# Dynamic convolution and gated projection on one core: another order of TensorE's products, and 32-column tiles for one of them, placed between the two halves of the convolution

## The chip, the cores and the metric

The kernel runs on one core of a Trainium2 chip. The metric is the device time of one execution in microseconds, median of several runs; lower is better. Engines are named as in the profile: PE is TensorE, PEld its weight loads, DVE VectorE, ACT ScalarE, POOL GpSimd; SP issues DMAs.

## The reference

Batch 8, sequence 4224, width 192, all float32. Cut to what is computed:

```
w   = softmax(weight_gen, axis=-1)               # (8, 4224, 8 heads, 7 taps)
x1[b,s,h,:] = sum_k w[b,s,h,k] * xpad[b,s+k,h,:] # causal, 24 channels per head
gate = sigmoid(sum_j conv_w[j,c] * x1pad[b,s+j,c])   # 5 taps per channel, causal
out  = (gate * (x1 @ w_val)) @ w_out             # 192 x 192 each
```

## The kernel before, in words

The sequence is cut into groups of 120 positions (88 in the first, 56 in the last); two groups make a *pair*, and 19 pairs, counted by `q`, go through three steps, one round apart. All work is recorded at hand-written times: `at(t, fn)` puts an entry on a list, and the list sorted by time is the program's order. In round `q`, `st(off, ...)` records at `when(q) + off`; a round is 24.5 units long (18 for `q` = 2). An entry's time is only its place in the order; on the chip every engine takes its own instructions in that order and waits on semaphores.

In round `q`:

- *Convolution of pair q* (`bank`, L343): eight banks of sixteen products, four banks for each group. Each product has 126 rows and 32 columns of weights, in one of four column positions. Two banks go to the PSUM tile `ps[0]`, two to `ps[1]`. ScalarE copies each bank out (`evac`, L358: `S`, `ringB`, `ringA` twice). GpSimd's DMAs (`move`) then bring rows from `S` to their places in `ringA` and `ringB`.
- *First taps of pair q* on ScalarE (`tap0`, L384), late in the round.
- *Gate and value of pair q-1*. VectorE adds four taps of `aA` and four of `aB` (`tap`, L388); ScalarE applies the sigmoid to each (`sigm`, L393). PE makes the value products in four parts, here by the size of tile (rows x columns of PE's array): `wvm_` (L415, 128 x 32, to `ps[2]`), `wva_` (L420, 128 x 128, two pieces, to `ps[0]` and `ps[1]`), `wvd_` (L426, 64 x 64, to `ps[2]`), `wvb_` (L432, 64 x 128, added to `wva_`'s pieces). VectorE multiplies gate and value (`gv`): L439 reads `ps[0]`, then `ps[1]`; L444 and L447 read `ps[2]`.
- *Output of pair q-2* in four pieces: `omA` (L455, 128 x 128) and `omB` (L464, 64 x 128) add up in one PSUM tile, ScalarE copies it out (`oev`, L470), SP stores it (`store`, L478). Piece 0 is written to `ps[3]` early in the round, the others late. The tile of a piece is `bk[i]`; `tA`, `tB`, `tE` are the places of `omA`, `omB` and `oev`.

The softmax weights are made in parts of 2048 positions, about one part in two rounds. One kind of round, called *X* here, has the exponential on ScalarE (L223: a load of another function table, then the function; after it the sigmoid L393 needs a table load too), and sum, reciprocal and product on VectorE (L227 to L249). The other kind, *Y*, has SP's copies of halo rows (`halo`, L241, after the product L249), ScalarE's four copies that spread the weights (`spread`, L261, after the halo copies have landed), and maximum and difference on VectorE (L215, L219). SP also issues per round 18 loads of these weights for the next pair (L317) and, by turns, four stores (L272) or four loads (L206).

What writes into a PSUM tile waits for the engine that read its last contents. In the order before, `ps[1]` and `ps[2]` carry the last two output pieces, so these wait for `gv`; the next round's convolution needs `ps[0]` from `gv` and `ps[1]` from a copy of `oev`.

Of the kernel before, what the change touches and what calls it, by code (L numbers as in the profile page):

```python
# [16 lines left out]
def tile_dynconv_gated_moe(  # L17
# [91 lines left out]
    def at(t, fn, *args):  # L109
        plan.append((t, len(plan), fn, args))  # L110
# [72 lines left out]
    class Softmax:  # L183
# [29 lines left out]
        def max(self):  # L213
            w, m = self.own()
            nc.vector.tensor_reduce(out=m, in_=w, axis=AX.X, op=ALU.max)  # L215
# [287 lines left out]
    def when(q):  # L503
        return WHEN[q] if q < 4 else WHEN[3] + TP * (q - 3)
# [99 lines left out]
    for p in parts[3:]:  # L604
        q = next(q.q for q in pairs if p.use < q.s + q.n)
# [17 lines left out]
    for q, pr in enumerate(pairs + [None, None]):  # L623
        p1 = pairs[q - 1] if 1 <= q <= NP else None
        p2 = pairs[q - 2] if q >= 2 else None
        t = when(q)

        def st(off, fn, *args):
            at(t + off, fn, *args)

        if pr:
            ng = len(pr.g)
            order = [(gi, kind) for gi in range(ng) for kind in (3, 2, 0, 1)]
            for i, (gi, kind) in enumerate(order):
                st(0.8 * i, pr.bank, gi, kind, i % 4)
                st(0.8 * i + 0.9, pr.evac, gi, kind, i % 4)
            m0 = [(k, u) for k in (4, 5) for u in range(2)]
            m1 = [(k, u) for u in range(2) for k in range(4)]
            for i, (k, u) in enumerate(m0 + m1):
                late = 0.8 * (4 * (ng - 1) + (1, 2, 3)[i // 4]) + (0.91 if q else 1.5)  # L640
                st(late + 0.001 * i, pr.move, k, u)
            for g in range(2):
                st((17.5, 11.0, 14.8)[min(q, 2)], pr.halo, g)
            st((17.6, 11.1, 15.9)[min(q, 2)], pr.tap0, 0, 0)
            st((17.7, 11.2, 17.0)[min(q, 2)], pr.tap0, 0, 1)
            st((17.8, 11.3, 19.6)[min(q, 2)], pr.tap0, 1)
        if q + 1 < NP:
            nx = pairs[q + 1]
            for gi, g in enumerate(nx.g):
                if q >= 1:  # L650
                    if g.n == NB:
                        st((0.0, 7.2)[gi], g.load_x, nc.gpsimd)
                    else:
                        st(7.2, lambda g=g: nc.gpsimd.memset(g.xb[:, :, :], 0.0))
                        st(7.3, g.load_x, nc.gpsimd)
                for i, (p, w, lo, hi) in enumerate(g.segments()):
                    tt = max(t + (3.5, 7.0)[gi], p.ready + 0.001 * (1 + gi))
                    if q == 0:
                        tt = 30.5 if p is s0 else (34.0, 37.0)[gi]
                    assert p.ready < tt < when(q + 1), (q, gi, tt, when(q + 1))  # L660
                    at(tt, g.load_t, p, w, lo, hi, (nc.sync, nc.scalar)[i % 2 if q == 0 else 0])
        if p1:
            E = range(p1.pieces)
            for j in range(1, KC):
                st((2.6 if q > 1 else 8.0) + 2.1 * (j - 1) * (1 if q > 1 else 0.1), p1.tap, 0, j)
                st((11.4 if q > 1 else 8.5) + 1.2 * (j - 1) * (1 if q > 1 else 0.1), p1.tap, 1, j)
            st(11.5 if q > 1 else 8.9, p1.sigm, 0)
            st(16.4 if q > 1 else 9.0, p1.sigm, 1)
            st(6.5, p1.wvm_)
            st(10.2, p1.wvd_)  # L670
            for e in E:
                st(8.2 + 0.8 * e, p1.wva_, e)
                st((15.0 if q > 1 else 10.3) + 0.8 * e, p1.wvb_, e)
                st((15.9 if q > 1 else 10.4) + 0.8 * e, p1.gv, 0, e)
                st((17.6 if q > 1 else 10.5) + 0.1 * e, p1.gv, 1, e)
        if p2:
            J2 = [(e, k) for e in range(p2.pieces) for k in range(2)]
            bk = (3, 3, 1, 2)
            tA = (2.9, 17.5, 18.9, 20.2)
            tB = (3.0, 16.7, 21.4, 22.0)  # L680
            tE = (3.35, 18.8, 21.95, 22.7)
            for i, (e, k) in enumerate(J2):
                af = tA[i] < tB[i]
                st(tA[i], p2.omA, e, k, bk[i], af)
                st(tB[i], p2.omB, e, k, bk[i], not af)
                st(tE[i], p2.oev, e, k, bk[i])
                st(tE[i] + 0.01, p2.store, e, k, nc.sync)
# [29 lines left out]
```

## Time and profile before

| | |
|---|---|
| median of 3 runs | 536.47 us (536.35 to 538.43) |
| the profiled execution's own time | 530.59 us |
| its span, first to last instruction | 528.8 us |
| mean granted TensorE clock | 0.942 |
| PE busy | 454.5 us, 86% |
| DVE busy | 427.1 us, 81% |
| ACT busy | 313.6 us, 59% |
| POOL busy | 317.3 us, 60% |

The profile is of one execution that took 530.59 us, 5.88 us less than the median. The span leaves out what lies before the first and after the last instruction (1.8 us). A share of busy time is an average over stages: the first 137 us fill the pipeline, then come 14 whole rounds, then the last short ones.

### The profile page before, as it was taken

The numbers are of one execution on the slowest core, as the hardware profiler recorded it, in microseconds if no ns is written. First come the engines' busy times: TensorE is split into PE (matmuls) and PEld (weight loads), VectorE is DVE, ScalarE is ACT, GpSimd is POOL, SyncE is SP. The second block draws the span as 40 slices with busy tenths as digits, with TensorE's granted clock in tenths as the row PEclk, the third lists the DMA queues.
The fourth block names the chain that finished last, engine by engine and source line by source line (L and its number), as shares of the span: only waits on it lengthen the run. The fifth ranks groups of instructions, "written<-read, shape, count | busy, mean of one in ns | idle before, by whom it ended". The sixth has DMA issues, their size and how long they took to land.

```text
span 528.8 us, 15980 instructions
## 1 busy us (share of the span) xinstructions
PE 454.5 (86%) x6546; PEld 330.2 (62%) x6546; DVE 427.1 (81%) x342; ACT 313.6 (59%) x433; POOL 317.3 (60%) x554
## 2 busy tenths in 40 slices
PE   7030674969999899999999999999998999999996
PEld 3030552556858485858676776768584868586584
DVE  6988346898979896999799979888995979595960
ACT  6432364658585748485858675767767575545532
POOL 9878256667474839293949382938566565807400
PEclk9565697879999999999999999999999999999999
DMA  7796749986979797879797978797797858654344
GB/s 222 212 307 187 202 110 254 244 234 175 248 218 281 196 270 195 270 195 269 208 288 201 267 199 263 202 259 220 219 254 220 256 149 251 177 165 100 92 113 111
DMA packets 86743, 112.42 MB, mean 213 GB/s; under 512 B 19133, under 2 KB 73796, under 8 KB 86542
## 3 DMA queue, kind: packets, MB, share of 16 engines
q1 hardware_dynamic: 62988, 70.86, 46.9%
q0 software_dynamic: 22560, 38.13, 28.1%
q10 hardware_dynamic: 1122, 2.40, 1.4%
q8 instruction: 52, 0.85, 0.6%
q14 instruction: 21, 0.17, 0.1%
HBM read 59.63 MB, written 42.43 MB: 193 GB/s over the span
## 4 chain that ended last, share of the span: by engine, by line
PE 44%; issue 15%; DMA 14%; POOL 13%; DVE 7%; ACT 5%; SPq 2%; ACTq 0%; POOLq 0%; DVEq 0%
PE ps L343 15%; PE ps L455 10%; POOL xt L286 6%; PE ps L464 6%; PE ps L420 5%; POOL ringA L366 4%; DMA xt<-in_x_dram 3%; PE ps L415 3%; PE ps L432 3%; POOL ringB L368 2%; DMA ringA<-S 2%; DMA tb<-z 2%; DMA ringB<-S 2%; PE ps L426 2%; DVE aB L447 1%
## 5 line engine op out<-in xcount | busy, mean ns | idle before, releaser
L343 PE MATMUL ps<-tb,xt 126*32 126x120 f32 (+2 forms) x4608 | 148.0, 286 | 62.3 <-DMA tb<-z 26.8
L343 PEld LDWEIGHTS ps<-tb,xt 126*32 126x32 f32 x4608 | 134.9, 115 | 74.5 <-issue 33.4
L388 DVE SCALAR_TENSOR_TENSOR aA<-ringA,wf,aA 128x1920 f32<-128x1920 f32 (+2 forms) x76 | 157.3, 2070 | 15.9 <-ACT aA L384 13.7
L286 POOL DMA_DIRECT2D xt<-in_x_dram x272 | 158.4, 597 | 17.8 <-DMA xt<-in_x_dram 5.0
L368 POOL DMA_DIRECT2D ringB<-S x76 | 42.1, 559 | 139.0 <-ACT ringB L358 113.0
L455 PE MATMUL ps<-wf,aA 128*120 128x192 f32 (+2 forms) x576 | 108.7, 336 | 5.9 <-DVE aB L447 3.9
L455 PEld LDWEIGHTS ps<-wf,aA 128*120 128x120 f32 (+2 forms) x576 | 91.2, 186 | 20.2 <-DVE aB L447 9.0
L470 ACT COPY ot<-ps 120x768 f32<-120x768 f32 (+2 forms) x72 | 56.0, 802 | 66.2 <-PE ps L464 55.2
L366 POOL DMA_DIRECT2D ringA<-S x152 | 82.0, 547 | 21.6 <-DMA ringB<-S 9.0
L388 DVE SCALAR_TENSOR_TENSOR aB<-ringB,wf,aB 128x960 f32<-128x960 f32 (+2 forms) x76 | 86.9, 1143 | 1.9
L439 DVE TENSOR_TENSOR aA<-ps,aA 128x960 f32<-128x960 f32 (+2 forms) x36 | 39.3, 1130 | 52.7 <-PE ps L432 33.1
L420 PE MATMUL ps<-ringA,wva 128*128 128x480 f32 (+2 forms) x144 | 61.8, 571 | 0.0
L464 PE MATMUL ps<-wf,aB 64*120 64x192 f32 (+2 forms) x576 | 59.7, 335 | 0.9 <-ACT ot L470 0.9
L358 ACT COPY S<-ps 128x480 f32<-128x480 f32 (+2 forms) x36 | 19.9, 552 | 63.2 <-PE ps L343 46.5
L464 PEld LDWEIGHTS ps<-wf,aB 64*120 64x120 f32 (+2 forms) x576 | 46.5, 182 | 16.8 <-issue 15.2
L358 ACT COPY ringA<-ps 128x480 f32<-128x480 f32 (+2 forms) x72 | 36.2, 554 | 33.7 <-PE ps L343 33.7
L384 ACT ACTIVATE aA<-ringA,wf 128x960 f32<-128x960 f32 (+2 forms) x38 | 39.2, 1033 | 22.9 <-DMA ringA<-S 22.7
L420 PEld LDWEIGHTS ps<-ringA,wva 128*128 128x128 f32 x144 | 25.8, 189 | 35.7 <-issue 22.2
L261 ACT COPY zt<-wt 128x512 f32<-128x512 f32 (+3 forms) x36 | 30.9, 936 | 5.7 <-DMA wt<-wt 3.2
L432 PE MATMUL ps<-ringB,wvb 64*128 64x480 f32 (+2 forms) x144 | 33.5, 581 | 0.0
L415 PE MATMUL ps<-ringA,wvm 128*32 128x480 f32 (+2 forms) x304 | 33.5, 537 | 0.0
L393 ACT ACTIVATE aA<-aA 128x1920 f32<-128x1920 f32 (+2 forms) x19 | 32.1, 1690 | 1.0 <-DVE aA L388 0.9
(62 smaller groups left out, 361.1 us busy)
## 6 DMA issues: line engine op xcount, KB each, us to landing
xt<-in_x_dram POOLq DMA_DIRECT2D x272, 94.5 KB, 3.7
out_dram<-ot SPq DMA_DIRECT2D x68, 360.0 KB
tb<-z SPq DMA_DIRECT2D x235, 74.4 KB
z<-zt SPq DMA_DIRECT2D x28, 306.0 KB
wt<-in_weight_gen_dram SPq DMA_DIRECT2D x28, 224.0 KB
ringA<-S POOLq DMA_DIRECT2D x136, 30.0 KB, 3.5
tb<-z SPq DMA_DIRECT2D x69, 52.1 KB
wt<-wt SPq DMA_DIRECT2D x9, 294.0 KB
```

What stands on the lines that cost most here:

```text
L286: eng.dma_start(out=self.xb[0:G * NW, j, 0:D], in_=src)
L343: nc.tensor.matmul(out=pa[Q * c:Q * c + Q, n * l:n * l + n], lhsT=g.xb[0:k, LH * u + l, C * h:C * h + Q], rhs=t[:, (LH * u + l) // LQ, PAD ...
L358: nc.scalar.copy(out=dst, in_=pa)
L366: nc.gpsimd.dma_start(out=ringA[q:q + h, LH * u:LH * u + LH, p0:p0 + n], in_=St[p:p + h, :, 0:n])
L368: nc.gpsimd.dma_start(out=ringB[HD * u + q:HD * u + q + h, :, p0:p0 + n], in_=St[p:p + h, :, 0:n])
L388: nc.vector.scalar_tensor_tensor(out=a, in0=self.src(g, j), scalar=cw[:, g, j:j + 1], in1=a, op0=ALU.mult, op1=ALU.add)
L415: nc.tensor.matmul(out=ps[2][c:c + Q, i, 0:self.w * self.pieces // 2], lhsT=wvm[:, Q * k:Q * k + Q], rhs=self.half(0, u, i), start=True, s ...
L420: nc.tensor.matmul(out=self.v01(e)[:, u], lhsT=wva, rhs=self.A(e, u), start=True, stop=False)
L432: nc.tensor.matmul(out=self.v01(e)[:, u], lhsT=wvb[hs], rhs=self.Bt(e)[hs], start=False, stop=True, tile_position=(HD * u, 0))
L455: nc.tensor.matmul(out=ps[b][0:n, u, D * t:D * t + D], lhsT=g[:, u, t], rhs=woa, start=first and t == 0, stop=not first, skip_group_check= ...
L464: nc.tensor.matmul(out=ps[b][0:n, u, D * t:D * t + D], lhsT=g[hs, t], rhs=wob[hs], start=first and t == 0, stop=not first, skip_group_chec ...
L470: nc.scalar.copy(out=ots[0:n, 2 * e + k], in_=ps[b][0:n, :, 0:2 * D])
```

## The change

In rounds from `q` = 2 on, the products of the value and output stand elsewhere in the order. `wvm_` goes from after the convolution to between its two groups. Output piece 0 goes from between the two groups to after `wva_`; its copy and store go with it. `wvb_` follows it, then `wvd_`. The last three output pieces have their three `omA` first and their three `omB` after, and two of them use `ps[0]` and `ps[1]` in place of `ps[1]` and `ps[2]`. No instruction is added or removed, apart from how they group.

```diff
-            st(6.5, p1.wvm_)
-            st(10.2, p1.wvd_)
+            st(2.9 if q > 1 else 6.5, p1.wvm_)
+            st(10.0 if q > 1 else 10.2, p1.wvd_)
             for e in E:
                 st(8.2 + 0.8 * e, p1.wva_, e)
-                st((15.0 if q > 1 else 10.3) + 0.8 * e, p1.wvb_, e)
+                st((9.8 if q > 1 else 10.3) + 0.01 * e, p1.wvb_, e)
                 st((15.9 if q > 1 else 10.4) + 0.8 * e, p1.gv, 0, e)
...
-            bk = (3, 3, 1, 2)
-            tA = (2.9, 17.5, 18.9, 20.2)
-            tB = (3.0, 16.7, 21.4, 22.0)
-            tE = (3.35, 18.8, 21.95, 22.7)
+            bk = (3, 3, 0, 1)
+            tA = (9.5, 18.0, 18.9, 20.2)
+            tB = (9.6, 21.6, 21.0, 21.3)
+            tE = (9.65, 21.65, 21.05, 21.35)
```

On PE, in a whole round of the middle, from the convolution's second group on (`tb1`; `ps0` to `ps3` are the PSUM tiles). Before:

```order
L343 MATMUL ps0_91<-tb1_64,xt0_72 32x120 x32
L343 MATMUL ps1_92<-tb1_64,xt0_72 32x120 x32
L415 MATMUL ps2_93<-ringA_75,wvm_86 32x480 x8
L420 MATMUL ps0_91<-ringA_75,wva_83 128x480 x2
L420 MATMUL ps1_92<-ringA_75,wva_83 128x480 x2
L426 MATMUL ps2_93<-ringB_76,wvd_85 64x480 x4
L432 MATMUL ps0_91<-ringB_76,wvb_84 128x480 x2
L432 MATMUL ps1_92<-ringB_76,wvb_84 128x480 x2
L464 MATMUL ps3_94<-wf_88,aB1_80 120x192 x4
L455 MATMUL ps3_94<-wf_88,aA_78 120x192 x4
L455 MATMUL ps1_92<-wf_88,aA_78 120x192 x4
L455 MATMUL ps2_93<-wf_88,aA_78 120x192 x4
```

And in the change, the same place:

```order
L343 MATMUL ps1_92<-tb1_64,xt0_72 32x120 x32
L420 MATMUL ps0_91<-ringA_75,wva_83 128x480 x2
L420 MATMUL ps1_92<-ringA_75,wva_83 128x480 x2
L455 MATMUL ps3_94<-wf_88,aA_78 120x192 x4
L464 MATMUL ps3_94<-wf_88,aB1_80 120x192 x4
L432 MATMUL ps0_91<-ringB_76,wvb_84 128x480 x2
L432 MATMUL ps1_92<-ringB_76,wvb_84 128x480 x2
L426 MATMUL ps2_93<-ringB_76,wvd_85 64x480 x4
L455 MATMUL ps3_94<-wf_88,aA_78 120x192 x4
L455 MATMUL ps0_91<-wf_88,aA_78 120x192 x4
L455 MATMUL ps1_92<-wf_88,aA_78 120x192 x4
L464 MATMUL ps0_91<-wf_88,aB1_80 120x192 x4
```

Output piece 0 (the first L455 and L464 here) came from between the convolution's groups; L415 went there. Before, the round ends with L464 to `ps1` and `ps2`; now with L464 to `ps0`, `ps1` and `ps3`.

On ACT, in a round of kind X, around the table loads. Before:

```order
L470 COPY ot_82<-ps3_94 120x768
L358 COPY S_77<-ps0_91 128x4x120
L358 COPY ringB_76<-ps0_91 128x4x120
L358 COPY ringA_75<-ps1_92 128x4x120 x2
L223 ACT_TABLE_LOAD
L223 ACTIVATE wt2_67<-wt2_67 128x2x896
L393 ACT_TABLE_LOAD
L393 ACTIVATE aA_78<-aA_78 128x1920
```

And in the change:

```order
L358 COPY S_77<-ps0_91 128x4x120
L358 COPY ringB_76<-ps0_91 128x4x120
L358 COPY ringA_75<-ps1_92 128x4x120 x2
L223 ACT_TABLE_LOAD
L223 ACTIVATE wt2_67<-wt2_67 128x2x896
L470 COPY ot_82<-ps3_94 120x768
L393 ACT_TABLE_LOAD
L393 ACTIVATE aA_78<-aA_78 128x1920
```

The copy of output piece 0 (L470) moved from ahead of the second group's copies to between the exponential and the sigmoid's table load. In a round of kind Y it moved to between the four copies L261 and the sigmoid.

On SP, where a round of kind X ends and one of kind Y begins. Before:

```order
L206 DMA wt2_67<-in_weight_gen_dram 32x2x896 x4
L478 DMA out_0_dram<-ot_82 120x2x384 x3
L241 DMA wt1_66<-wt1_66 112x2x336
L241 DMA wt1_66<-wt1_66 12x2x336
L478 DMA out_0_dram<-ot_82 120x2x384
L317 DMA tb0_63<-z0_97 14x4x238
```

And in the change:

```order
L478 DMA out_0_dram<-ot_82 120x2x384
L206 DMA wt2_67<-in_weight_gen_dram 32x2x896 x4
L478 DMA out_0_dram<-ot_82 120x2x384 x3
L241 DMA wt1_66<-wt1_66 112x2x336
L241 DMA wt1_66<-wt1_66 12x2x336
L317 DMA tb0_63<-z0_97 14x4x238
```

The store of output piece 0 moved from ahead of the 18 loads L317 to behind them. The order on DVE and on POOL is the same in both kernels.

## Rows read from the trace of the kernel before

**Rows 1.** Busy time in fourteen rounds: us, PE, PEld, DVE, ACT, POOL; clock; DMA.

```profile
137.15:489.55 352.40, 342.87 (x5042) 250.07 (x5040) 304.12 (x219) 228.99 (x309) 213.38 (x377) 1.00 0.80 223
```

**Rows 2.** Timeline of PE, one whole round (start, us, operation, count of records).

```profile
365.68 3.88 PE L343 MATMUL ps<-tb,xt 126*32 126x120 f32 x128
369.48 1.57 PE L455 MATMUL ps<-wf,aA 128*120 128x192 f32 x8
370.98 0.92 PE L464 MATMUL ps<-wf,aB 64*120 64x192 f32 x8
371.83 3.89 PE L343 MATMUL ps<-tb,xt 126*32 126x120 f32 x128
375.51 1.82 PE L415 MATMUL ps<-ringA,wvm 128*32 128x480 f32 x16
377.26 3.49 PE L420 MATMUL ps<-ringA,wva 128*128 128x480 f32 x8
380.68 1.04 PE L426 MATMUL ps<-ringB,wvd 64*64 64x480 f32 x8
381.64 1.88 PE L432 MATMUL ps<-ringB,wvb 64*128 64x480 f32 x8
383.36 0.82 PE L464 MATMUL ps<-wf,aB 64*120 64x192 f32 x8
384.11 4.48 PE L455 MATMUL ps<-wf,aA 128*120 128x192 f32 x24
388.51 1.57 PE L464 MATMUL ps<-wf,aB 64*120 64x192 f32 x16
390.01 1.24 PE L343 MATMUL ps<-tb,xt 126*32 126x120 f32 x36
```

**Rows 3.** Timeline of PE, near the end: three output pieces without a wait.

```profile
513.71 4.17 PE L455 MATMUL ps<-wf,aA 128*120 128x192 f32 x24
```

**Rows 4.** PE by line, fourteen rounds: busy, mean ns, idle before and releasers.

```profile
L343 PE MATMUL ps<-tb,xt 126*32 126x120 f32 x3584 | 110.1, 278 | 3.8 <-issue 3.6
L455 PE MATMUL ps<-wf,aA 128*120 128x192 f32 x448 | 84.9, 337 | 5.8 <-DVE aB L447 3.9 <-DVE aA L439 1.5
```

**Rows 5.** Timeline of DVE, a round X and the round Y after it.

```profile
257.18 2.22 DVE L439 TENSOR_TENSOR aA<-ps,aA 128x960 f32<-128x960 f32 x2 [2.86 <-PE ps L432]
...
267.44 8.97 DVE L388 SCALAR_TENSOR_TENSOR aA<-ringA,wf,aA 128x1920 f32<-128x1920 f32 x4
...
282.03 2.22 DVE L439 TENSOR_TENSOR aA<-ps,aA 128x960 f32<-128x960 f32 x2 [0.72 <-ACT aA L393]
...
290.18 4.47 DVE L388 SCALAR_TENSOR_TENSOR aA<-ringA,wf,aA 128x1920 f32<-128x1920 f32 x2
```

**Rows 6.** Timeline of ACT, a round X.

```profile
249.58 1.02 ACT L358 COPY ringA<-ps 128x480 f32<-128x480 f32 x2 [0.80 <-PE ps L343]
...
251.91 1.70 ACT L223 ACTIVATE wt<-wt 128x1792 f32<-128x1792 f32 x1
253.62 1.28 ACT L393 ACT_TABLE_LOAD   x1
254.92 1.80 ACT L393 ACTIVATE aA<-aA 128x1920 f32<-128x1920 f32 x1
```

**Rows 7.** Timeline of ACT, the round Y of rows 2.

```profile
371.95 0.81 ACT L470 COPY ot<-ps 120x768 f32<-120x768 f32 x1 [1.32 <-PE ps L464]
373.93 0.56 ACT L358 COPY S<-ps 128x480 f32<-128x480 f32 x1 [1.17 <-PE ps L343]
```

**Rows 8.** Timelines of DVE, SP and ACT, another round Y.

```profile
163.41 2.03 DVE L249 TENSOR_TENSOR wt<-wt,mx 128x1792 f32<-128x1792 f32 x1
...
168.24 2.49 SPq L241 DMA_DIRECT2D wt<-wt  x2
...
175.94 3.77 ACT L261 COPY zt<-wt 128x512 f32<-128x512 f32 x4 [2.56 <-DMA wt<-wt]
```

**Rows 9.** ACT by line, fourteen rounds: busy, mean ns, idle before and releasers.

```profile
L261 ACT COPY zt<-wt 128x512 f32<-128x512 f32 (+3 forms) x24 | 21.2, 959 | 5.1 <-DMA wt<-wt 2.6 <-DMA out_dram<-ot 1.3 <-DVE aB L388 1.2
```

## The prediction, before the run

> **What bounds the kernel now.** I began with busy time by stretch. In the fourteen whole rounds between 137.15 and 489.55 us PE is busy 342.87 of 352.40 us at a clock of 1.00, which is 2.4 GHz; DVE 304.12, ACT 228.99 [rows 1]. So PE is the bound there, with 9.5 us idle, and a round takes 352.40 / 14 = 25.17 us. The timeline of PE then shows what a round is made of [rows 2]: its rows overlap by less than 0.1 us, so a step's length is the distance to the next row's start. In microseconds: convolution 3.80, output piece 0 in 1.50 + 0.85, convolution 3.68, value products 1.75 (L415), 3.42 (L420), 0.96 (L426), 1.72 (L432), output 0.75, 4.40, 1.50. Sum 24.33: the round without a stall. 14 x 24.33 = 340.6, so stalls cost 11.8 us in all. PE by line names most of them [rows 4]: 5.8 us before L455, on DVE, and 3.8 us in the convolution, nearly all "issue", a wait whose cause the trace doesn't show. DVE is not far behind: from the gate products of a round X at 257.18 to the start of the next taps at 267.44 it needs 10.26; taps take until 281.31 (282.03 less 0.72 idle), 13.87; in the round Y gate products and softmax take 290.18 - 282.03 = 8.15 [rows 5]. For X and Y together that is 10.26 + 8.15 + 2 x 13.87 = 46.15, or 23.08 a round.
>
> **What a change of tiling costs.** The 24 records of L455 near the end took 4.17 - 0.08 (the overlap) = 4.09 [rows 3]; 8 records with a change before and after took 1.50 [rows 2]. So 16 cost 2.59, 8 cost 1.295, and a change on both sides 0.205. L464 says the same: 16 records 1.50, 8 records 0.85, so 0.65 and 0.20; and after L432, which has the same tiling, 8 records took 0.75: one change, 0.10 at each end. The convolution takes 0.12 less when L415, also of 32 columns, follows (3.68 against 3.80).
>
> Per round I count nine changes before, and six after: into L420, L464, L426, L455, L464, L343. The new round, in its order: convolution 3.68; L415 1.75 - 0.10 = 1.65; convolution 3.75 (3.80 less an entry, not separately shown, between 0 and 0.10, taken as 0.05); L420 3.32; L455 1.40; L464 0.75; L432 1.72 (its change moves from entry to exit); L426 0.96; three L455 4.09; three L464 3 x 0.65 + 0.20 = 2.15. Sum 23.47. Against 24.33 that is 0.86 less: 0.55 for tilings, and 0.31 because three L455 took 4.40 and not 4.09: the third waited for `ps[2]`, which L447 reads last. The last pieces now use `ps[0]` and `ps[1]`, which L439 frees before L447 is done with `ps[2]`.
>
> **What takes the place of PE.** If PE ran without a stall, a round would be 23.47. It doesn't, because the copy of output piece 0 now stands on ACT directly ahead of the sigmoid. ACT takes its work in order: before, it sat idle 1.32 us for piece 0 and 1.17 for the copy behind it [rows 7].
>
> Round X. L464 of piece 0 ends 3.68 + 1.65 + 3.75 + 3.32 + 1.40 + 0.75 = 14.55 after the round's start. Its copy started 371.95 - 371.83 = 0.12 after that point before [rows 2, 7]: 14.67. ACT would be free by about 13.3: the second convolution ends at 9.08, then 1.02 of copies, 1.28, 1.70 and some 0.2 of signals [rows 6]. The copy (0.81 [rows 7], less some 0.09 by which rows of one engine overlap) lets the next instruction go at 15.39, the table load (1.28, plus 0.02) at 16.69, the sigmoid (1.80) at 18.49, and the first L439 (half of 2.22, with a signal at each end) at 19.68. PE reaches the second L455 of the late three, in `ps[0]`, at 14.55 + 1.72 + 0.96 + 0.10 + 1.30 = 18.63. It waits 1.05 and loses 0.10 in loading weights anew: the round takes 24.62. Before, exponential, table load and sigmoid followed each other without that copy [rows 6].
>
> Round Y. DVE starts the gate products of X at 18.53 and is ready for the next after 10.26 + 13.87 = 24.13, which is 18.04 in Y. ACT is in time: L261 takes 3.77 [rows 8] and may start at 10.2, after the convolution's copies; if it starts by 11.7, copy and sigmoid are done by 18.0. So L439's first half ends at 19.2, PE waits 0.57 and 0.10: 24.14.
>
> X and Y together take 48.76, before 2 x 24.33 = 48.66. The tilings' gain is thus paid back where both kinds of softmax work occur. Rounds without it exist: L261 has 24 records, four to a round [rows 9], so of fourteen rounds six are Y, six X and two plain. Plain rounds have neither wait: 23.47, a gain of 0.86 each. The last softmax part has 8 rows a partition in place of 16, so in its Y DVE is early: about 0.6 gained. Sum: five pairs +0.5, the last X +0.3, its Y -0.6, two plain -1.7: **-1.5 us**.
>
> **Stalls.** Of 5.8 us before L455, 3.9 ended with L447 [rows 4]. That place is gone: after L447 comes only `wvm_`, in the next round. Where the cause was a late sigmoid, the wait returns at L439; I take half of the 5.8 as gone, **-2.9**, with 0 and -3.9 as ends. "Issue" stays: 3.8, perhaps less where PE would wait for DVE anyway (0.67 in Y): **-0.5**, with 0 and -1.5.
>
> **Start and end.** Until 137 us PE waits for loads; nothing is taken there. The last three short rounds have fewer changes too, 0.55 and less each: **-1.0**, with 0 and -1.6.
>
> SP's loads for the next pair start sooner, because piece 0's store no longer stands ahead of them; they landed in time before, so nothing is taken. ACT's first copies of a round now wait for nothing new; PE's first bank waits for the copy of piece 2, which takes 0.12 + 0.81 beside the 1.40 of L464 behind it.
>
> **Sum:** -1.5 - 2.9 - 0.5 - 1.0 = -5.9. On the profiled execution's own 530.59 that is 524.7; the median of the runs is 536.47, 5.88 higher, so I set the difference against the median: **530.5**, 1.1% less.
>
> **A rule weighed.** The trace has the sigmoid's table load begin 0.01 after the exponential ends, and the sigmoid 0.02 after the load [rows 6]; I price the switch at 1.28. The Trainium skill, ScalarE: Activation LUTs, section What ACT_TABLE_LOAD costs, gives 1.28 for the load and adds a drain of 1.38 to every switch. With that, as an estimate from its figures, six rounds X would each be 1.38 longer, and the sum +2.4 in place of -5.9. No row here has such a gap.
>
> **Rivals.**
>
> *All of it arrives.* ACT isn't late, PE never waits for L439: 14 x 0.86 + 5.8 + 1.0 = 18.8 less, 517.7. For it: PE bounds the stretch [rows 1]. Against: ACT waited in order for piece 0 [rows 7]. It would need the table load to pass a waiting copy. By the Trainium skill, TensorE: Matmul & The Clock Gate, ScalarE's queue is strictly first in, first out (table at the top); the rows agree. Chance 0.05.
>
> *No change.* The waits on L447 all come back at L439, because DVE has no more than 1.3 us a round to spare (24.38, the mean of X and Y, less 23.08), and each "issue" stall ahead of piece 0 delays copy, sigmoid and gate alike. Then -1.5 - 1.0 remain, less a microsecond of new waits: 535. Chance 0.27.
>
> *Slower.* The halo copies. In one round Y they landed 175.94 - 165.44 = 10.50 after the softmax product L249 [rows 8]; in the other five the four copies L261 waited 2.5 us in all [rows 9]. Now L249 ends 18.53 + 10.26 - 24.62 = 4.17 into Y. L261 behind 10.50 starts at 14.67, copy and sigmoid end at 20.97, and gate products start 2.9 later than the 18.04 above. The point that decides is 18.04 - 1.80 - 0.72 - 3.77 = 11.75, or 7.6 after L249. If all six take 10.5, that adds 17: 547; with a mean of 9.5, 11: 542. Against it: 2.80 of the 10.50 passed before the copies were issued [rows 8], behind three stores that now have about a microsecond more of time to go out before L249 ends; 7.7 is left, close to the point. Chance 0.15.
>
> **How the numbers follow.** Half a per cent, 2.7 us, is about what a measurement tells from no change. The forecast has 0.53 (its own range 526 to 533.5). Faster: it and the first rival, 0.58. Same 0.27. Slower 0.15. The range leaves out the first rival and the upper half of the last: 525.5 to 538.5.
>
> **What would show it.** Right: PE's round has six changes, L464 after L420 and L455; before the second of the late L455 idle time released by DVE L439, some 1 us in rounds X; no idle time released by L447; ACT's L470 released by PE directly ahead of L393. Wrong: rounds X at 23.5 (ACT not late), or DVE idle in Y for L393 behind L261.

## The result, and the profile after

The change takes 538.19 us (median of 20 runs, 534.74 to 541.24), the kernel before, run beside it, 536.34 (20 runs, 530.40 to 541.69). The ratio of the two is 1.0078 [1.0053, 1.0103]: slower by 0.8%, where 1.1% faster was forecast, and just inside the range. The ratio is taken from the fast runs alone and isn't the quotient of these two medians, which is 1.0034. The profiled execution took 541.24 us, its span 539.5. It is the slowest of the twenty, and the profile of the kernel before, of 530.59 us, is of one near its fastest: two profiles show where the time went, but their difference, 10.65 us, is more than the change costs.

The same fourteen whole rounds as in [rows 1], now from 141.57 to 500.11: us, PE, PEld, DVE, ACT, POOL, clock, DMA share, GB/s.

```profile
141.57:500.11 358.54, 338.81 (x5042) 255.36 (x5040) 303.79 (x218) 226.74 (x309) 213.52 (x377) 0.99 0.79 219
```

PE has 4.1 us less to do than before, and its rounds take 6.1 us more. One plain round shows the first half of that, in the timeline of PE (start, us, operation, count), against [rows 2]. (L415 had tiles of 32 columns before too; only its place is new.)

```profile
476.64 3.88 PE L343 MATMUL ps<-tb,xt 126*32 126x120 f32 x128
480.31 1.82 PE L415 MATMUL ps<-ringA,wvm 128*32 128x480 f32 x16
481.92 3.86 PE L343 MATMUL ps<-tb,xt 126*32 126x120 f32 x128
485.72 3.49 PE L420 MATMUL ps<-ringA,wva 128*128 128x480 f32 x8
489.04 1.46 PE L455 MATMUL ps<-wf,aA 128*120 128x192 f32 x8
490.44 0.92 PE L464 MATMUL ps<-wf,aB 64*120 64x192 f32 x8
491.19 1.77 PE L432 MATMUL ps<-ringB,wvb 64*128 64x480 f32 x8
492.90 1.03 PE L426 MATMUL ps<-ringB,wvd 64*64 64x480 f32 x8
493.86 4.17 PE L455 MATMUL ps<-wf,aA 128*120 128x192 f32 x24
497.96 2.22 PE L464 MATMUL ps<-wf,aB 64*120 64x192 f32 x24
500.11 0.40 PE L343 MATMUL ps<-tb,xt 126*32 126x56 f32 x13
```

From start to start it takes 500.11 - 476.64 = 23.47 us, to the hundredth what was forecast for a round without a stall. (Two steps miss, L415 by 0.04 down and the second half of the convolution by 0.05 up, and cancel.) But 14 x 23.47 is 328.6, so 29.9 us of stalls are in the fourteen rounds, where 11.8 were before. PE by line names 19.7 of them (busy, mean ns, idle before and releasers); they answer to [rows 4].

```profile
L343 PE MATMUL ps<-tb,xt 126*32 126x120 f32 x3584 | 112.2, 278 | 6.3 <-issue 6.3
L455 PE MATMUL ps<-wf,aA 128*120 128x192 f32 x448 | 84.1, 340 | 12.0 <-DVE aA L439 8.0 <-ACT ot L470 3.9
L420 PE MATMUL ps<-ringA,wva 128*128 128x480 f32 x112 | 49.0, 579 | 1.4 <-issue 1.4
```

L447 is gone as a releaser. In its place stand three things: waits for L439, one wait for L470, and twice as much "issue" (7.7 us in place of 3.6). The idle column holds less than a stall costs. Taken from the distances between steps, less those of the plain round above, the late L455 lost 17.2 us and the convolution with L420 12.7.

**Rounds X.** Timelines of ACT, DVE and PE in one of them.

```profile
157.73 0.80 ACT L470 COPY ot<-ps 120x768 f32<-120x768 f32 x1 [1.55 <-PE ps L464]
158.55 1.28 ACT L393 ACT_TABLE_LOAD   x1
159.84 1.80 ACT L393 ACTIVATE aA<-aA 128x1920 f32<-128x1920 f32 x1
...
161.68 2.22 DVE L439 TENSOR_TENSOR aA<-ps,aA 128x960 f32<-128x960 f32 x2 [4.27 <-ACT aA L393]
...
160.19 1.57 PE L455 MATMUL ps<-wf,aA 128*120 128x192 f32 x8
162.89 2.87 PE L455 MATMUL ps<-wf,aA 128*120 128x192 f32 x16 [1.13 <-DVE aA L439]
```

ACT waits 1.55 us for piece 0, copies it, loads the table, and applies the sigmoid; DVE has then waited 4.27; and the second late L455, in `ps[0]`, waits 1.13 us for DVE. All six rounds X show this wait, 1.13 to 1.14 each, and the step takes 5.50 instead of 4.10.

**One round Y** took 31.4 us, from 216.92 to 248.32. Timelines of DVE, SP, ACT and PE in it, as [rows 8].

```profile
219.09 2.02 DVE L249 TENSOR_TENSOR wt<-wt,mx 128x1792 f32<-128x1792 f32 x1
...
217.68 3.02 SPq L206 DMA_DIRECT2D wt<-in_weight_gen_dram  x4
220.79 2.95 SPq L478 DMA_DIRECT2D out_dram<-ot  x3
223.83 2.45 SPq L241 DMA_DIRECT2D wt<-wt  x2
226.38 9.96 SPq L317 DMA_DIRECT2D tb<-z  x10
...
215.74 2.21 ACT L470 COPY ot<-ps 120x768 f32<-120x768 f32 x3 [0.91 <-PE ps L464]
...
233.61 3.71 ACT L261 COPY zt<-wt 128x512 f32<-128x512 f32 x4 [6.46 <-DMA wt<-wt]
237.22 0.80 ACT L470 COPY ot<-ps 120x768 f32<-120x768 f32 x1
237.91 1.81 ACT L393 ACTIVATE aA<-aA 128x1920 f32<-128x1920 f32 x1
...
239.75 2.22 DVE L439 TENSOR_TENSOR aA<-ps,aA 128x960 f32<-128x960 f32 x2 [4.86 <-ACT aA L393]
...
238.07 1.98 PE L455 MATMUL ps<-wf,aA 128*120 128x192 f32 x8 [3.85 <-ACT ot L470]
240.97 5.28 PE L455 MATMUL ps<-wf,aA 128*120 128x192 f32 x16 [0.91 <-DVE aA L439]
```

The product L249 ended at 221.11, but SP had just begun with the three stores, and issued the halo copies at 223.83 to 226.28. They landed 12.5 us after L249's end. In [rows 8] that was 10.50. The issue came as late after L249 as there, 2.72 us against 2.80; what grew is the time from issue to landing, 9.78 us against 7.70. L261 waited 6.46 for them, and copy and sigmoid stood behind L261, DVE behind the sigmoid, PE behind both.

**The end** came 39.35 us after the last whole round, before 39.25. The last two pieces, of 56 positions, both wait for the copy of an earlier piece, which has the same tile `ps[3]`; in the kernel before only the last one waited, 0.93 us (timeline of PE in the change):

```profile
529.96 1.51 PE L455 MATMUL ps<-wf,aA 128*56 128x192 f32 x8 [1.00 <-ACT ot L470]
...
533.20 1.51 PE L455 MATMUL ps<-wf,aA 128*56 128x192 f32 x8 [0.93 <-ACT ot L470]
```

**The start.** The first whole round began at 141.57, in [rows 1] at 137.15. That need not be the change's: a second profile of the kernel before took 534.0 us, had its whole rounds from 142.48 on, and these took 350.5, with issue waits of 2.1 us.

### The profile page after: what moved, and what is told of

The parts are those of the page before. It is cut to its first block, busy times and chain, and to the rows that moved or that the text cites. A ratio compares the mean times of both kernels' runs of the same rounds, so it can differ in the third digit from the quotient of the medians.

```text
span 539.5 us, 16074 instructions
## 1 busy us (share of the span) xinstructions
PE 449.7 (83%) x6546; PEld 336.7 (62%) x6546; DVE 428.0 (79%) x342; ACT 310.9 (58%) x433; POOL 317.7 (59%) x554
## 5 line engine op out<-in xcount | busy, mean ns | idle before, releaser
L343 PE MATMUL ps<-tb,xt 126*32 126x120 f32 (+2 forms) x4608 | 150.1, 286 | 69.0 <-DMA tb<-z 22.4
L343 PEld LDWEIGHTS ps<-tb,xt 126*32 126x32 f32 x4608 | 137.8, 115 | 86.4 <-issue 42.6
L455 PEld LDWEIGHTS ps<-wf,aA 128*120 128x120 f32 (+2 forms) x576 | 95.4, 190 | 38.6 <-issue 19.4
L455 PE MATMUL ps<-wf,aA 128*120 128x192 f32 (+2 forms) x576 | 107.0, 338 | 14.1 <-DVE aA L439 8.0
L470 ACT COPY ot<-ps 120x768 f32<-120x768 f32 (+2 forms) x72 | 54.2, 805 | 68.5 <-PE ps L464 66.1
L439 DVE TENSOR_TENSOR aA<-ps,aA 128x960 f32<-128x960 f32 (+2 forms) x36 | 39.3, 1130 | 62.4 <-ACT aA L393 34.8
L420 PE MATMUL ps<-ringA,wva 128*128 128x480 f32 (+2 forms) x144 | 62.6, 577 | 1.4 <-issue 1.4
L464 PE MATMUL ps<-wf,aB 64*120 64x192 f32 (+2 forms) x576 | 57.0, 335 | 0.0
L358 ACT COPY ringA<-ps 128x480 f32<-128x480 f32 (+2 forms) x72 | 36.2, 554 | 31.1 <-PE ps L343 31.1
L464 PEld LDWEIGHTS ps<-wf,aB 64*120 64x120 f32 (+2 forms) x576 | 45.4, 183 | 8.9 <-issue 8.8
L420 PEld LDWEIGHTS ps<-ringA,wva 128*128 128x128 f32 x144 | 26.3, 193 | 28.5 <-issue 24.6
L261 ACT COPY zt<-wt 128x512 f32<-128x512 f32 (+3 forms) x36 | 30.8, 934 | 10.3 <-DMA wt<-wt 9.7
L415 PE MATMUL ps<-ringA,wvm 128*32 128x480 f32 (+2 forms) x304 | 34.4, 547 | 0.0
L432 PE MATMUL ps<-ringB,wvb 64*128 64x480 f32 (+2 forms) x144 | 31.6, 555 | 0.0
```

What stands on the lines that cost most here:

```text
L343: nc.tensor.matmul(out=pa[Q * c:Q * c + Q, n * l:n * l + n], lhsT=g.xb[0:k, LH * u + l, C * h:C * h + Q], rhs=t[:, (LH * u + l) // LQ, PAD ...
L358: nc.scalar.copy(out=dst, in_=pa)
L420: nc.tensor.matmul(out=self.v01(e)[:, u], lhsT=wva, rhs=self.A(e, u), start=True, stop=False)
L439: nc.vector.tensor_tensor(out=a, in0=self.v01(e), in1=a, op=ALU.mult)
L455: nc.tensor.matmul(out=ps[b][0:n, u, D * t:D * t + D], lhsT=g[:, u, t], rhs=woa, start=first and t == 0, stop=not first, skip_group_check= ...
L464: nc.tensor.matmul(out=ps[b][0:n, u, D * t:D * t + D], lhsT=g[hs, t], rhs=wob[hs], start=first and t == 0, stop=not first, skip_group_chec ...
```

## The experiments

Three theories came out of the profile after. **S**: the copy of piece 0 ahead of the sigmoid holds sigmoid, L439 and the late pieces. **H**: the halo copies come too late in rounds Y. **F**: PE's instructions don't come fast enough when the convolution's halves stand close together ("issue"). Each ratio is to the kernel before, run beside it. Idle times are those of the fourteen whole rounds.

### The copy of piece 0 behind the sigmoid

```diff
-            tE = (9.65, 21.65, 21.05, 21.35)
+            tE = (11.6, 21.65, 21.05, 21.35)
```

> The change with one number other: the copy of output piece 0 stands on ACT behind the sigmoid of aA, no longer ahead of it. PE's order is that of the change. Theory S (the copy holds up the sigmoid, so DVE's first gate product and with it PE's late output pieces): the idle time before L455 released by DVE L439, 1.13 us in each round X of the change (8.0 us in all), goes below 1 us in all, rounds X fall from 24.8 to 23.5, the whole to 530 us or less. Theory F (PE runs out of instructions because the two halves of the convolution now stand closer): the waits called issue stay near 7.7 us in the rounds, and if they are the main loss the time stays near 538. Theory H (late halo copies, by chance): time near 538, and a round Y of 7 us more can come again.

538.0 us, ratio 1.0041 [0.9998, 1.0084]. PE by line:

```profile
L343 PE MATMUL ps<-tb,xt 126*32 126x120 f32 x3584 | 112.4, 278 | 9.7 <-issue 9.2 <-ACT ot L470 0.5
L455 PE MATMUL ps<-wf,aA 128*120 128x192 f32 x448 | 84.7, 346 | 9.0 <-ACT ot L470 9.0
```

Not one wait for L439 is left, and undisturbed rounds X come down to 23.5 to 23.7: S holds for them. The time hardly follows. Two rounds Y took 31.1 and 31.3 us, since the copy now stands behind a sigmoid that stands behind late halo copies, and issue waits were 10.6 (9.2 here, 1.4 before L420), on the same order of PE that had 7.7 above.

### The halves next to each other

```diff
-            st(2.9 if q > 1 else 6.5, p1.wvm_)
+            st(6.5, p1.wvm_)
```

> The change with the 128x32 value products (L415) back behind the convolution, so that its two halves follow each other with nothing between. Six tilings as in the change. Theory F: 512 short instructions in a row in place of 2 x 256 with 1.6 us between; the waits called issue grow from 7.7 us to 10 or more, time 2 to 4 us over that of the change (540 to 542). Theory S: ACT's order is unchanged, rounds X keep the wait of 1.13 us, time as the change, 538 within 1 us.

542.85 us, ratio 1.0115 [1.0075, 1.0155]; waits for L439 7.1 us, issue waits 12.4, in these two rows of PE by line:

```profile
L343 PE MATMUL ps<-tb,xt 126*32 126x120 f32 x3585 | 110.6, 279 | 10.2 <-issue 10.1
L415 PE MATMUL ps<-ringA,wvm 128*32 128x480 f32 x224 | 29.4, 584 | 2.3 <-issue 2.3
```

So moving L415 between the halves didn't make the stalls. Whether it took some away is less sure: 12.4 stands against 7.7 and 10.6, each from one execution, and the interval of the ratio meets the change's.

### Piece 0 back between the halves

```diff
-            tA = (9.5, 18.0, 18.9, 20.2)
-            tB = (9.6, 21.6, 21.0, 21.3)
-            tE = (9.65, 21.65, 21.05, 21.35)
+            tA = (2.95, 18.0, 18.9, 20.2)
+            tB = (3.0, 21.6, 21.0, 21.3)
+            tE = (3.35, 21.65, 21.05, 21.35)
```

> The change with output piece 0, its copy and store back between the halves of the convolution, behind the 128x32 products. That makes nine changes of tiling again. Theory S: no wait for L439 in rounds X (7 us less), and three changes of tiling more in each of 17 rounds (0.55 each, 9 us more): about 540. Theory F adds a gain: with 4 us of slow products between the halves the waits called issue fall back to about 4 us, 4 us less: about 536. Both wrong: 547 (only the tilings).

535.32 us, ratio 1.0013 [0.9981, 1.0045]. (This kernel and the next change the output of the first pair's second piece; the instructions are the same.) With the halves 4.1 us apart, issue waits are 2.1 us. The time is near the 536 that S and F gave together, but not for their reason: S wanted no wait for L439 in rounds X, and waits for L439 are 9.5. In five of six rounds X they are 0.74 each, though the copy no longer stands ahead of the sigmoid: the second half now begins 7.8 us into the round in place of 5.3, and ACT's copies, exponential, table load and sigmoid follow it without a gap. The longer ones, up to 3.0, lie in rounds Y.

### The new late pieces alone, then only in the middle

On the kernel before, first in all rounds (these four lists in place of the old ones), then in whole rounds alone:

```diff
+            if 3 <= q < NP - 1:
+                bk = (3, 3, 0, 1)
+                tA = (2.9, 18.0, 18.9, 20.2)
+                tB = (3.0, 21.6, 21.0, 21.3)
+                tE = (3.35, 21.65, 21.05, 21.35)
```

> The kernel before with the last part of the change alone: the late output pieces use ps[0] and ps[1], their three L455 first and their three L464 after. Nine changes of tiling as before; ACT's copy of piece 0 early, as before. The prediction's step: each round loses 0.31 us of waiting for L447, and the 3.9 us of idle time released by it go: 4 to 8 us less than before, about 530. If these waits only move to DVE L439: as before, 536.

> The kernel before with the new late output pieces (ps[0] and ps[1], three L455 then three L464) in the rounds 3 to 16 alone; start and end keep the old order. Halves of the convolution stay apart, the early copy stays early. e4 had clean rounds of 24.0 in place of 24.33, but 1.9 us more in the last rounds (two waits of 1.08 us for a copy of ACT) and 12 us of late halo copies. If the last rounds were what e4 lost: 2 to 5 us below before, 531 to 534. If shorter rounds are paid back in late halo copies: as before, 535 to 537.

In all rounds: 536.79 us, ratio 1.0048 [1.0014, 1.0081]. In the middle alone: 532.81, ratio 0.9964 [0.9934, 0.9994], 0.4% below the kernel before, with an interval that just leaves out 1. Clean rounds took 24.0 in both, 0.31 less than in [rows 2], as worked out: no wait for L447 is left. The end took 41.1 in the first and 39.28 in the second, so the new order costs 1.9 us in the short rounds. Issue waits were 1.6 and 4.5. What is left are rounds Y of up to 30 us; L261 waited 11.7 us in the second kernel.

### Halo copies ahead of the stores

The halo copies' entry goes some 7 units earlier, on the kernel just shown and, with the old lists in the short rounds and the copy behind the sigmoid, on the change:

```diff
-        at(when(q - 2) + 3.3, p.halo, (SP,))
+        at(when(q - 3) + 20.9, p.halo, (SP,))
```

> As e5, and SP issues the halo copies (L241) ahead of the three stores of the late pieces. Theory H (halo copies that land late hold up L261, behind it the sigmoid, the gate products and PE): they are issued 2 to 4.5 us sooner after L249, idle time before L261 goes from some 10 us to under 3, 3 to 8 us less than e5: 526 to 530. If the lateness comes from the copies' own time on the DMA queues and not from their place: as e5.

> The change with the copy of output piece 0 behind the sigmoid (as e1), the halo copies ahead of the three stores (as e6), and start and end in the old order of output pieces. Theories S and H answered, F not: no idle time for L439, L261 or L470 to speak of, clean rounds of 23.5, issue waits still 8 to 11 us in the rounds; 9 to 11 us less than the change, 527 to 530. If F is small: 522 to 525.

533.11 us, ratio 0.9974 [0.9936, 1.0013], and 534.4, ratio 0.9995 [0.9955, 1.0035]. ACT by line in the first:

```profile
L261 ACT COPY zt<-wt 128x512 f32<-128x512 f32 (+3 forms) x24 | 21.2, 967 | 0.4 <-DMA out_dram<-ot 0.4
```

The wait of 11.7 us is gone, and with it the waits for L439 (6.2 to 0.5). The time did not follow, for PE then waited elsewhere, 2.7 us for a transfer of `z`. In the second it waited 4.2 us for the next pair's weights, and 9.5 on issue.

### L426 between the halves as well

On the change; on the last kernel above; and on that with the halo copies in their old place:

```diff
-            st(10.0 if q > 1 else 10.2, p1.wvd_)
+            st(2.95 if q > 1 else 10.2, p1.wvd_)
```

> The change, with one edit: L426 (0.97 us of products of 64 x 64) goes from after L432 to behind L415, between the halves of the convolution, which are then some 2.6 us apart in place of 1.6. F, the supply of PE's instructions: issue waits in the fourteen whole rounds fall from 7.7 us to 4 or less, as where the halves are 2.35 us apart (2.2 to 4.8). A stall in L426 itself would be counted to issue as well. Against F, if issue waits come by chance or by what DVE and DMA do at that time: 6 or more. S unchanged: sigmoid's copy order is the same, but the second half of the convolution ends about 1.0 later, and PE has 0.97 less to do between it and the late pieces, so the wait for L439 in rounds X stays near 1.1 plus up to 1.0. Price: one change of tiling more, 0.1 a round, so clean rounds of 23.6. H unchanged. Time: 0 to 4 us less than the change, ratio to the kernel before 1.000 to 1.008.

> The kernel with the copy of piece 0 behind the sigmoid, halo copies first and the old lists in the first and last short rounds (534.4 measured, ratio 0.9995, issue waits 9.5 us), with L426 between the halves as well. If S, H, the end and F are the four causes, and no fifth takes their place: issue waits 4 or less, 5 us gone, 529 to 530, ratio 0.988 to 0.993. If the cost only moves on (loads of the weights for the next pair, which PE waited 4.2 us for there, or ACT behind the later second half): ratio 0.997 to 1.002.

> As the run before it, with the halo copies at their old place. H says: rounds Y of 26 to 31 us come back in two or more of six, 5 to 10 us more than with the halo copies first, ratio 1.000 to 1.008. If the halo copies ahead of the stores only move the wait to the loads for the next pair: within 2 us of it, and those waits (4.2 us) are gone.

On the change: 548.1 us, ratio 1.0255 [1.0204, 1.0305], 9.9 us more than the change where 0 to 4 less were expected. PE by line and, under it, PE's timeline in the round X that was shown above for the change:

```profile
L343 PE MATMUL ps<-tb,xt 126*32 126x120 f32 x3585 | 110.9, 278 | 1.6 <-issue 1.3
L455 PE MATMUL ps<-wf,aA 128*120 128x192 f32 x448 | 84.1, 337 | 18.1 <-DVE aA L439 18.1
```

```profile
157.68 1.78 PE L432 MATMUL ps<-ringB,wvb 64*128 64x480 f32 x8
159.38 1.57 PE L455 MATMUL ps<-wf,aA 128*120 128x192 f32 x8
163.05 2.87 PE L455 MATMUL ps<-wf,aA 128*120 128x192 f32 x16 [2.10 <-DVE aA L439]
```

PE now has 0.97 us less to do between piece 0 and the late pieces, and waits 2.10 instead of 1.13: 0.97 more. The eight other rounds, where the change had 0.30 or nothing when undisturbed, now all wait 0.68 or 0.69. That is S in its plainest form: from the end of piece 0 on, the chain copy, table load, sigmoid, L439 has a length of its own, and work taken off PE there comes back as idle time.

With the copy behind the sigmoid and the halo copies first: 531.39 us, ratio 0.9950 [0.9916, 0.9984], the lowest ratio here, though its interval meets those of the late pieces in the middle alone and of the kernel without this edit (0.9995). With the halo copies in their old place: 537.3, ratio 1.0058 [1.0025, 1.0091]. Only the place of these copies differs, and the two intervals don't meet: H is worth 1.1% there. L261 by line, of the one and then of the other:

```profile
L261 ACT COPY zt<-wt 128x512 f32<-128x512 f32 (+3 forms) x24 | 21.1, 963 | 0.8 <-DMA wt<-wt 0.8
```

```profile
L261 ACT COPY zt<-wt 128x512 f32<-128x512 f32 (+3 forms) x24 | 21.1, 957 | 8.2 <-DMA wt<-wt 5.3 <-DMA tb<-z 2.9
```

For F it was a miss. With the halves 2.7 us apart issue waits should have been 4 us or less; they were 2.1 in the first kernel, but 8.3 and 8.1 in the other two. Distance alone doesn't decide. L343 of the kernel with the halo copies first (0.5 more came before L420):

```profile
L343 PE MATMUL ps<-tb,xt 126*32 126x120 f32 x3585 | 110.2, 278 | 9.8 <-issue 7.8 <-DMA wt<-in_weight_gen_dram 1.0 <-DMA out_dram<-ot 0.9
```

### Less DMA traffic

The packets of the instruction queue in the trace gave another reason. All eight issue stalls of the change end 2.2 to 2.6 us after such a packet starts. The one that started at 305.37, 2.45 us before PE went on at 307.82, is the only one from 305 to 308 us in the part on DMA queues (packets, MB, share of 16 engines):

```profile
q8 instruction: 1, 0.02, 1.9%
```

The kernel before had the same. Its three issue stalls, at 199.34, 323.69 and 401.68 us, end 2.4 us after such a packet starts. The longest of them in the timeline of PE, and then the only instruction packet from 399 to 402 us, which starts at 399.23:

```profile
401.68 0.30 PE L343 MATMUL ps<-tb,xt 126*32 126x120 f32 x1 [1.65 <-issue]
```

```profile
q8 instruction: 1, 0.02, 2.1%
```

So the trace that the prediction read could have named this wait. In the change, the busy share of the DMA engines (last number but one) in the two microseconds before three of the eight packets:

```profile
354.60:356.60 2.00, 2.00 (x40) 0.94 (x34) 1.96 (x2) 1.02 (x2) 0.68 (x2) 1.00 1.11 307
432.20:434.20 2.00, 2.00 (x79) 2.00 (x73) 1.97 (x2) 0.24 (x1) 0.00 (x0) 1.00 0.99 307
458.20:460.20 2.00, 2.00 (x80) 2.00 (x72) 1.96 (x3) 1.02 (x2) 0.00 (x0) 1.00 0.98 347
```

Before all eight the engines were full, 0.89 to 1.12; before the other 32 packets of this queue in the whole rounds 0.80 in the mean. Full engines alone don't make a stall, for 12 of these 32 had 0.97 or more. Theory **D**: the packets come late because the engines are full. So the loads of x were left out, on the change, on the kernel with the halves next to each other, and on the one of 531.39 us:

```diff
                     if g.n == NB:
-                        st((0.0, 7.2)[gi], g.load_x, nc.gpsimd)
+                        if q < 3:
+                            st((0.0, 7.2)[gi], g.load_x, nc.gpsimd)
```

> The change without the sixteen loads of x that POOL issues in each round, from q = 3 on (the convolution then works on the x of earlier groups, so the output of all later groups is not the reference's; the same instructions run on PE). DMA moves some 25 MB less of 112. D, the packets of PE's instructions come late because the sixteen DMA engines are full at that time: issue waits in the fourteen whole rounds fall from 7.7 us to 2 or less, and the L343 rows of the second half come back to 3.7 to 3.8. F in its first form, the halves stand too close whatever DMA does: 6 to 10. S doesn't depend on it: wait of about 1.1 for L439 in each X round stays. H should be gone, for the halo copies meet emptier queues. Time, whole rounds: D 337 to 341 us of 358.5, F 344 to 350.

> The kernel with the two halves of the convolution next to each other (issue waits 12.5 us), without the loads of x from q = 3 on, as in the run before. D: 2 or less. F in its first form: 10 to 13, since PE takes 512 records in 7.5 us there at whatever DMA traffic.

> The kernel with copy behind the sigmoid, halo copies first and L426 between the halves (issue waits 8.3 us, whole rounds 350.4), without the loads of x from q = 3 on. D: issue waits 2 or less, whole rounds of 23.6 to 24.4 throughout, 14 of them 332 to 338 us. F: issue waits 6 or more, 343 or more.

PE by line, L343 of the three in this order:

```profile
L343 PE MATMUL ps<-tb,xt 126*32 126x120 f32 x3585 | 110.6, 278 | 2.5 <-issue 2.5
```

```profile
L343 PE MATMUL ps<-tb,xt 126*32 126x120 f32 x3584 | 108.9, 278 | 5.8 <-issue 5.7
```

```profile
L343 PE MATMUL ps<-tb,xt 126*32 126x120 f32 x3585 | 108.8, 278 | 2.3 <-ACT ot L470 2.3
```

All issue waits: from 7.7 to 2.5 (halves 1.6 us apart), from 12.4 to 6.2 (next to each other), from 8.3 to none (2.7 apart). With less traffic most of them go, and the distance still counts: neither D nor F alone fits, since D asked for 2 or less in the second kernel. These are single executions, and leaving out the loads also takes work from POOL, which issues them (213.5 us busy in the change's fourteen rounds, 94.8 in the first of these); no run separates the traffic from that. The fourteen rounds took 344.1, 349.9 and 338.7 us; D had forecast 337 to 341 and 332 to 338 for the first and the third. In the first, rounds X without an issue wait take 24.9 and most rounds Y 24.0: forecast were 24.62 and 24.14. Its last two rounds take 23.5. So this is the change as the prediction saw it, once PE gets its instructions.

## Why the prediction was wrong, point by point

- **Tilings: right.** A clean round takes 23.47, as summed; the 0.31 from L447 were right as well, shown apart by the late pieces alone.
- **Rounds X: the mechanism was right, the size short.** Forecast was 1.05 of waiting and 0.10 of loading weights; 1.13 and 0.27 were measured, six times, 1.5 us in all. The table switch was rightly priced at 1.28: the load begins 0.02 after the copy, the sigmoid 0.01 after the load. There is again no drain of 1.38, which the Trainium skill, ScalarE: Activation LUTs, section What ACT_TABLE_LOAD costs, adds.
- **"'Issue' stays: 3.8": the step that failed.** With it, losses outside L455 would have been 5.5 us (11.8 of stalls before, less the 5.8 named at L455, less 0.5). They were 12.7: 7.2 us off. The prediction took a wait whose cause the trace didn't name for a constant. It is a wait for PE's own instructions, and it depends on what surrounds the 256 short products of a round: 3.6 and 2.1 us in two profiles of the kernel before, 7.7 and 10.6 in the two with the change's order on PE throughout.
- **The halo copies: the "slower" rival, half right.** Its argument against itself, that the three stores have a microsecond more of time to go out before L249 ends, was wrong: they went out at 220.79 to 223.74, L249 ended at 221.11. SP, and not the buffer they store, was late: ACT had copied the three pieces by 217.95, but SP issued four loads (L206) until 220.70. So the 2.8 before the issue stayed, and the 7.7 left after it, taken as it was, came out as 9.78, past the 7.6 where the delay begins to count. One round Y of six paid the price in the profiled execution, 7.9 us at L455. The forecast for L455 was 13.4 in all (10.5 of new waits, 2.9 left of the old); 17.2 came.
- **The end: forecast -1.0, measured +0.1.** One of the late pieces and the next round's piece 0 share `ps[3]`, and in the last short rounds little or nothing lies between them. The prediction had counted only the tilings there.
- The sum: 328.6 + 13.4 + 5.5 = 347.5 was forecast for the whole rounds, 328.6 + 17.2 + 12.7 = 358.5 measured: 11.0 more, and 1.1 at the end. By the ratio the change costs 4.2 us (by the medians 1.9) where 5.9 were to be gained, 10.1 off; two profiles of single executions can't be expected to agree with that more closely.
- The cures point the same way. The copy behind the sigmoid, old lists at the ends and halo copies first bring 1.0078 to 0.9995; with L426 between the halves it is 0.9950, a step that the two intervals don't make sure; less traffic takes the rest of the issue waits there, with one execution of 517.5 beside 533.8 of the kernel before.

**Open:** why the halo copies took 9.78 us to land in that round Y. Why issue waits are 2.1 in one kernel with L426 between the halves and 8.3 and 8.1 in the others. In the first PE waits 0.7 to 2.1 in each round before the late pieces, which could give the packets time; no run separates that. How often a round Y comes late differs among executions, and one profile of each kernel can't tell its mean.

## What to carry to other kernels

Work that is moved off the bounding engine saves only as far as the chain that it released follows: work out where each copy stands in its engine's order, and which later wait hangs on it. An idle time that the profile names only "issue", amid many short instructions, is no constant; look at the instruction queue's packets and at what the DMA engines do just before them. And an engine that issues DMAs with hardly a gap can pass a delay on to its next customer: here, with the halo copies first, PE waited 2.7 us for `z` in one kernel and 4.2 us for the next pair's weights in another, waits that it had not had with them in their old place.

## What was not expected of the hardware

PE can run dry of instructions. In the change's fourteen rounds 40 packets of 16 KB came in by the instruction queue q8 for 10,082 records of PE and PEld, about 252 a packet; a half of the convolution uses up 256 in 3.7 us. The Trainium skill, Runtime: NRT & Kernel Launch, section Instruction fetch mechanics, says that engines fetch their instructions in blocks of 16 KiB, 256 instructions, by a DMA queue of their own, and that the cost of crossing a block is mostly hidden. Size and queue agree for PE; a second instruction queue, q14, has packets of 8 KB here. Hidden it is in the kernel without loads of x and with 2.7 us between the halves (no issue wait); with all traffic and the halves next to each other 12.4 us of idle time in fourteen rounds were put down to issue.
